# An attention in front of two feed-forward layers: scores in two rounds of 288 tokens beside pieces of v_m @ w_in, and attention groups tied between whole steps of the first product

## The chip, the cores and the metric

One core of one Trainium2 chip runs the whole program. The metric is device time in microseconds. Times are compared as medians of several runs. The profile is of one profiled execution; its times count from the start of its span.

## What is computed

Eight batches of eight heads, 576 tokens, head size 64, with 32 memory slots per head, go through an attention over the memory. The result, a matrix of 4608 tokens by 512, goes through two feed-forward layers with a hidden size of 2048.

```python
a = phi - np.max(phi, axis=2, keepdims=True); a = np.exp(a)
a = a / (np.sum(a, axis=2, keepdims=True) + 1e-09)
k_m = np.einsum('bhsm,bhsd->bhmd', a, k)
v_m = np.einsum('bhsm,bhsd->bhmd', a, v)
scores = scale * np.matmul(q, k_m.transpose(0, 1, 3, 2))
...
attn = attn / (np.sum(attn, axis=-1, keepdims=True) + 1e-09)
return np.matmul(attn, v_m).astype(np.float32)
...
h = x @ w_in; r = np.maximum(h, 0.0); g = r * r       # layer 1
h = x @ w_in; g = h * (1.0 / (1.0 + np.exp(-h)))      # layer 2
return (g @ w_out).astype(np.float32)
```

The layers' weights arrive as 64-bit words and are turned into fp32 on the chip.

## The kernel before, in words

The program has four stages, one after the other on TensorE: the attention with the first layer's `w_in` (lines up to L499, here called the front), then three large products that are not touched by the change: the first layer's `w_out` (L677), the second layer's `w_in` (L796) and its `w_out` (L677 again).

In the front, attention and `x @ w_in` are merged: since x is attn @ v_m per head, x @ w_in is attn @ (v_m @ w_in). So for each batch the kernel forms v_m @ w_in in four **pieces** of 512 hidden columns (`piece`, TensorE into `pswp` at L378) and multiplies them with the transposed attention `at`. That is the **first product** (`first_product`, into `h` at L482): 16 **steps** per batch, each one a block of 128 hidden units, 12 matmuls of 288 tokens (two halves of the 576 tokens by six). ScalarE evicts each step with a Relu into `gt` (L491). Two PSUM tiles `h` alternate.

While the 16 steps of one batch run, the attention of the next batch is done in small **groups** of matmuls between them, which here is called a cycle:

- the softmax over tokens of phi: `pm` (L316, two transposes for the maximum) and `psmx` (L325);
- k_m and v_m: `pskv` (L343, 40 matmuls 128 rows by 32 columns of the array, two groups of 20), then scaled and turned: `pst` (L365, two transposes twice) and copied to `kvm`;
- scores: `scores(r)` for rounds r = 0, 1, 2 of RT = 192 tokens: `pssc` (L378, 8 matmuls on 64 rows by 32 columns), then on VectorE two transposes of 32x32 blocks out of PSUM (L389), the row maximum, a subtraction, an exponential on ScalarE (L393), the sum, its reciprocal and the scaling (L397, on GpSimd from batch 1 on);
- `transpose_attn(r)`: a transpose (L406), the rounding to the upper part on ScalarE (L409), the rest by a subtraction (L410); the tile `et` between them has one buffer;
- the four pieces, `pswp`, split into an upper part by ScalarE (L420) and a rest by VectorE (L421).

All these small PSUM tiles come from one pool `bg` of two buffers. The `h` matmuls use the whole 128x128 array, as do `pm`, `psmx` and `pst`; the others use parts of it.

The order comes from two places. `PLAN` and `PLAN1` (L47 to L54) say ahead of which step each part is written, and a scheduler that runs when the program is built then moves instructions on each engine by its own simulated times. It may put a group into the middle of a step, or cut a group in two. On the chip each engine works through its list in order. `hold` ties the issue of background work to the start of a step.

Beside this, VectorE, ScalarE and the DMA queue of SyncE convert `w_out` of the first layer in the background (L146 to L198, tiles `st`, `pw`, `pp`), from step 20 on, one part per step; `g1` takes the outputs of the steps.

At the start, batch 0's attention has no first product to run beside; its three score rounds (all on VectorE, the first subtraction L410 on GpSimd) stand between the conversions of `w_in` (`unit`, L146 to L149).

Of the kernel before, what the change touches and what calls it, by code (L numbers as in the profile page):

```python
# [8 lines left out]
F32 = mybir.dt.float32  # L9
# [9 lines left out]
P = 128  # L19
# [3 lines left out]
NP = H // 2  # L23
HALF = S // 2
NF = DFF // P
NC = 5
NR = 3
RT = S // NR
# [18 lines left out]
PLAN = {  # L47
    "phi": -15, "kv": (-13, -11, -9, -7), "softmax": (-9, -6, -4), "product": (-1, 0), "turn": (2, 3),
    "q": (-5, -3, 6), "scores": (5, 7, 10), "attn": (7, 9, 12), "pieces": (5, 9, 13, 17),
}  # L50
PLAN1 = {
    "phi": -47, "kv": (0, 0, 1, 2), "softmax": (2, 4, 5), "product": (6, 7), "turn": (8, 9),
    "q": (3, 4, 10), "scores": (9, 11, 13), "attn": (11, 13, 15), "pieces": (10, 12, 14, 16),
}  # L54
# [15 lines left out]
def attention_moe_moe(ctx: ExitStack, tc, q, kv, phi, w_in1, w_out1, w_in2, w_out2, out):  # L70
# [18 lines left out]
    nc = tc.nc  # L89
# [24 lines left out]
    def hold(ins, until=10 ** 6, step=-1):  # L114

        if begun and len(begun) < until:
            after(ins, begun[step])

    def after(ins, other):
# [132 lines left out]
    def unit(j, i):  # L252
        ins = to_f32(win[:, j, 2 * i:2 * i + 2].rearrange("p k c -> p (k c)"), staged[j, i])
        if begun:
            hold(ins)
        elif j > 1:
            after(ins, ready[min(j, 4) - 2])

# [4 lines left out]
    def front(b):  # L263
# [26 lines left out]
        def load_q(r):  # L290
            if b == 0 and r == 2:
                t = gpool.tile([P, 2, S], F32, tag="gt", name="q")
                t = t.rearrange("p a n -> p (a n)")[:, :NP * RT].rearrange("p (k n) -> p k n", k=NP)
            else:
                t = fpool.tile([P, NP, RT], F32, tag="q", bufs=2, name="q")
            st["q", r] = t
            hold(nc.sync.dma_start(t, q[b, r]))
# [38 lines left out]
        def kv_product(g):  # L336

            ps = st["ps", g] = bank("pskv")[:, 0, :2 * D + 1]
            for c in range(NC):
                n = rows(c)  # L340
                for p in range(NP):
                    h = 2 * p + g
                    nc.tensor.matmul(  # L343
                        ps[p * M:(p + 1) * M], st["a"][:n, c, h * M:(h + 1) * M], st["kv"][:n, p, c, g],
                        start=(c == 0), stop=(c == NC - 1),
                    )

# [13 lines left out]
        def kv_turn(g):  # L361
            y = st["y", g]
            pst = st["pst", g] = bank("pst")[:, 0, :2 * P].rearrange("p (s n) -> p s n", s=2)
            for i in range(2):
                nc.tensor.transpose(pst[:, i], y[:, i].rearrange("p s d -> p (s d)"), ident)  # L365

            if g == 0:
                st["kvm"] = fpool.tile([P, 2, P], F32, tag="kvm", name="kvm")
            d = slice(g * D, (g + 1) * D)
            nc.vector.tensor_copy(st["kvm"][d], st["pst", g][d])  # L370

        def by_heads(ps, s, x):

            for g in range(2):
                d = slice(g * D, (g + 1) * D)
                for p in range(NP):
                    m = slice(p * M, (p + 1) * M)
                    nc.tensor.matmul(ps[m, g], st["kvm"][d, s, m], x(p)[d], start=True, stop=True)  # L378

# [76 lines left out]
        for g in range(2):  # L456
            at(begin + plan["product"][g], lambda g=g: (kv_product(g), kv_scale(g)))
            at(begin + plan["turn"][g], lambda g=g: kv_turn(g))
# [14 lines left out]
    def first_product(t):  # L473
# [4 lines left out]
        for half in range(2):  # L478
            tk = slice(half * HALF, (half + 1) * HALF)
            ops = [(g, s, x) for g in range(2) for s, x in ((0, 0), (0, 1), (1, 0))]  # L480
            for k, (g, s, x) in enumerate(ops):
# [4 lines left out]
                if half == k == 0:  # L486
                    begun.append(mm)
        if f % 2 == 0:
            gts[b] = gpool.tile([P, 2, S], F32, tag="gt", name="gt")
# [402 lines left out]
```

## Time and profile before

| | us |
|---|---|
| median of 3 runs (1430.03 to 1431.23) | 1431.19 |
| span of the profiled execution | 1426.6 |
| PE busy / DVE busy / ACT busy / POOL busy | 1377.4 / 1035.2 / 789.6 / 37.0 |
| front, up to the first matmul of L677 | 346.7 |
| mean granted TensorE clock | 0.996 |

The profile gives no time of its own for the profiled execution beyond the span; the runs' median is 4.6 us over that span. PE is TensorE's matmuls, DVE VectorE, ACT ScalarE, POOL GpSimd, SPq the DMA queue of SyncE. Matmuls overlap in the pipeline, so a row's duration is longer than the time until the next row starts; the distances between the starts of rows say what a group takes on TensorE. A matmul on fp32 data appears as two records where the program has one instruction (pssc x16 is a group of eight); the `h` matmuls on rounded fp32 appear once.

### The profile page before, as it was taken

What the parts mean: (1) busy time and instruction counts of PE and PEld (TensorE: products, weight loads), DVE (VectorE), ACT (ScalarE), POOL (GpSimd) and SP (SyncE); (2) the same over time, 40 slices, a digit from 0 to 9 for tenths busy, and PEclk for the clock granted to TensorE, in tenths of its full rate; (3) what the DMA queues carried; (4) which work ended last, traced back from release to release, by engine and by line L of the source; (5) the groups of instructions that cost most, each with busy time, mean ns of one, the idle gap of its engine ahead of it and who ended that gap; (6) DMA issues with size and microseconds to landing.
All of it is one profiled execution on the core that took longest, in us unless ns stands there. A gap on an engine that the chain in (4) does not pass through costs nothing.

```text
span 1426.6 us, 25453 instructions
## 1 busy us (share of the span) xinstructions
PE 1377.4 (97%) x9264; PEld 1305.5 (92%) x9264; DVE 1035.2 (73%) x1809; ACT 789.6 (55%) x1329; POOL 37.0 (3%) x52
## 2 busy tenths in 40 slices
PE   3899999999999999999999999999999999999999
PEld 1677878788899999999999999999998999999998
DVE  6867878772798978889957677566538768678583
ACT  3566666666767585775545455455444444444443
POOL 1210000000000000000000000000000000000000
PEclk9999999999999999999999999999999999999999
DMA  9769999889779787798998887888999575665740
GB/s 344 248 223 338 324 329 313 290 291 393 240 231 314 226 288 252 255 290 290 336 336 279 303 303 275 286 275 297 348 399 345 161 256 173 226 223 161 239 152 34
DMA packets 208829, 388.25 MB, mean 272 GB/s; under 512 B 19264, under 2 KB 91456, under 8 KB 208704
## 3 DMA queue, kind: packets, MB, share of 16 engines
q1 hardware_dynamic: 208704, 386.62, 80.0%
q8 instruction: 73, 1.20, 0.3%
q14 instruction: 52, 0.43, 0.1%
HBM read 253.38 MB, written 133.17 MB: 271 GB/s over the span
## 4 chain that ended last, share of the span: by engine, by line
PE 75%; DVE 10%; DMA 9%; ACT 3%; issue 2%; SPq 0%; POOL 0%; ACTq 0%; DVEq 0%; POOLq 0%
PE psa L677 21%; PE psa L796 14%; PE h L482 11%; PE psc L677 11%; PE psc L796 7%; PE psb L677 4%; PE psb L796 4%; DMA r<-g 3%; DVE c L649 3%; PE pswp L378 2%; DMA st<-moe_w_out 1%; PE pskv L343 1%; DMA ws<-w1o 1%; ACT c L648 1%; DVE r L642 1%
## 5 line engine op out<-in xcount | busy, mean ns | idle before, releaser
L649 DVE TENSOR_TENSOR c<-r,c 128x768 fp32r<-128x768 f32 x336 | 318.9, 958 | 162.4 <-ACT c L648 160.7
L677 PE MATMUL psa<-c,ws 128*128 128x384 f32 x2304 | 418.2, 339 | 11.4 <-DVE c L649 9.0
L677 PEld LDWEIGHTS psa<-c,ws 128*128 128x128 f32 x2304 | 405.1, 190 | 15.6 <-DVE c L649 12.3
L648 ACT CAST c<-r 128x768 fp32r<-128x768 f32 x336 | 277.4, 834 | 215.7 <-PE psa L677 106.9
L482 PEld LDWEIGHTS h<-at,wp 128*128 128x128 f32 x1536 | 209.3, 190 | 53.5 <-ACT gt L491 20.2
L482 PE MATMUL h<-at,wp 128*128 128x288 f32 x1536 | 230.0, 303 | 12.4 <-ACT at L409 7.9
L796 PE MATMUL psa<-xc,ws 128*128 128x384 f32 x1152 | 218.4, 336 | 0.0
L677 PE MATMUL psc<-c,ws 128*128 128x384 f32 x1152 | 207.0, 336 | 2.8 <-ACT c L648 2.8
L677 PEld LDWEIGHTS psc<-c,ws 128*128 128x128 f32 x1152 | 201.2, 188 | 3.1 <-ACT c L648 3.1
L796 PEld LDWEIGHTS psa<-xc,ws 128*128 128x128 f32 x1152 | 202.1, 188 | 0.6 <-ACT u L563 0.3
L491 ACT ACTIVATE gt<-h 128x576 f32<-128x576 f32 x128 | 82.4, 649 | 52.4 <-PE h L482 49.4
L796 PE MATMUL psc<-xc,ws 128*128 128x384 f32 x576 | 110.8, 335 | 0.0
L677 PE MATMUL psb<-c,ws 128*128 128x384 f32 x576 | 105.4, 337 | 1.2 <-DVE c L649 1.1
L186 ACT CAST pp<-pw 128x256 fp32r<-128x256 f32 x148 | 58.6, 404 | 85.3 <-DMA w2o<-pp 31.2
L677 PEld LDWEIGHTS psb<-c,ws 128*128 128x128 f32 x576 | 100.4, 188 | 2.6 <-DVE c L649 2.5
L796 PEld LDWEIGHTS psc<-xc,ws 128*128 128x128 f32 x576 | 100.8, 188 | 0.0
L624 ACT ACTIVATE r<-r 128x768 f32<-128x768 f32 x96 | 79.8, 844 | 30.9 <-DMA r<-g 29.6
L187 DVE TENSOR_TENSOR pp<-pw,pp 128x256 f32<-128x256 f32 x148 | 61.3, 421 | 45.1 <-ACT pp L186 43.9
L810 ACT ACTIVATE g2t<-g2t 128x1152 f32<-128x1152 f32 x48 | 55.0, 1163 | 29.4 <-DVE g2t L561 27.0
L146 ACT ACTIVATE pw<-st 128x256 f32<-128x256 f32 x96 | 40.5, 433 | 39.9 <-DMA st<-moe_w_out 22.3
L796 PE MATMUL psb<-xc,ws 128*128 128x384 f32 x288 | 56.7, 335 | 0.0
L563 ACT COPY u<-psa 128x384 f32<-128x384 f32 x72 | 33.7, 475 | 38.8 <-DVE g2t L561 25.1
(86 smaller groups left out, 1202.1 us busy)
## 6 DMA issues: line engine op xcount, KB each, us to landing
r<-g SPq DMA_DIRECT2D x192, 384.0 KB, 5.0
g<-g2t SPq DMA_DIRECT2D x48, 768.0 KB, 7.0
ws<-w2i SPq DMA_DIRECT2D x136, 256.0 KB, 5.0
ws<-w2o SPq DMA_DIRECT2D x136, 256.0 KB, 3.7
ws<-w1o SPq DMA_DIRECT2D x116, 256.0 KB, 4.7
g<-gt SPq DMA_DIRECT2D x64, 384.0 KB, 5.5
kv<-kv SPq DMA_DIRECT2D x32, 516.0 KB, 6.9
st<-moe_w_out SPq DMA_DIRECT2D x64, 256.0 KB, 4.8
```

The lines of the kernel that those rows point to most:

```text
L146: ins = nc.scalar.mul(f.bitcast(F32), w1.bitcast(F32), 2.0 ** -112)
L186: held(nc.scalar.copy(hi, w[:, of]))
L187: tt(lo, w[:, of], hi.bitcast(F32), op=ALU.subtract)
L482: mm = nc.tensor.matmul(h[:, half, :HALF], wp[b, j][:, g, s, fo:fo + P], attnT[b][:, x, g, tk], start=(k == 0), stop=(k == len(ops) - 1),)
L491: nc.scalar.activation(gt[:, f % 2].rearrange("p (h t) -> p h t", h=2), h[:, :, :HALF], AF.Relu)
L563: nc.scalar.copy(s("u1"), t["a"])
L624: nc.scalar.activation(raw[b, name, h], raw[b, name, h], AF.Square)
L648: nc.scalar.copy(c[:, 0], r(name))
L649: tt(c[:, 1], r(name), c[:, 0].bitcast(F32), op=ALU.subtract)
L677: mm = nc.tensor.matmul(ps[o][bank], W[h * QS + u][:, slot(n), wi, o * P:(o + 1) * P], x[:, xi, u], start=(n in FIRST and h == u == m == 0 ...
L796: mm = nc.tensor.matmul(ps[q][bank], W[q][:, slot(n), wi, k * P:(k + 1) * P], x[:, xi, k], start=(n in FIRST and k == 0 and m == 0), stop= ...
L810: nc.scalar.activation(gq[q][:, :3], gq[q][:, :3], AF.Silu)
```

## The change

Scores come in two rounds of 288 tokens instead of three of 192; 288 is also half of the first product's tokens. `PLAN` puts each round at the step of a piece (5 and 9), so that `scores` and `piece` are written one behind the other. For batches 2 and on, each group of the attention is tied by a dependency without a semaphore: its first matmul comes after the last matmul of the step before it, and the next step's first matmul comes after the group's last. So a tied group is neither cut nor put inside a step. `pm` and `psmx` are not tied. The load of q for batch 0 no longer borrows a `gt` tile, and the scratch for dynamic DMA in SBUF is set to 1024 bytes, which makes room for the larger q, e and et tiles.

```diff
-NR = 3
+NR = 2
 RT = S // NR
...
 PLAN = {
-    "phi": -15, "kv": (-13, -11, -9, -7), "softmax": (-9, -6, -4), "product": (-1, 0), "turn": (2, 3),
-    "q": (-5, -3, 6), "scores": (5, 7, 10), "attn": (7, 9, 12), "pieces": (5, 9, 13, 17),
+    "phi": -15, "kv": (-13, -11, -9, -7), "softmax": (-9, -6, -4), "product": (-1, -1), "turn": (3, 3),
+    "q": (-5, 3), "scores": (5, 9), "attn": (8, 12), "pieces": (5, 9, 13, 17),
 }
 PLAN1 = {
...
-    "q": (3, 4, 10), "scores": (9, 11, 13), "attn": (11, 13, 15), "pieces": (10, 12, 14, 16),
+    "q": (3, 4), "scores": (10, 12), "attn": (12, 14), "pieces": (10, 12, 14, 16),
 }
...
+    ended = []
+    between = []
+
+    def between_steps(mms):
+
+        first, last = mms[0], mms[-1]
+        follow(first, between[-1] if between else ended[-1])
+        between.append(last)
+
+    def follow(ins, other):
+        tc.add_manual_dep(
+            ins.ins, other.ins.name,
+            mybir.DependencyInfo(mybir.DependencyClass.NoSync, mybir.DependencyReason.SCHED_ONLY), reason="follow",
+        )
...
         def load_q(r):
-            if b == 0 and r == 2:
-                t = gpool.tile([P, 2, S], F32, tag="gt", name="q")
...
+            t = st["q", r] = fpool.tile([P, NP, RT], F32, tag="q", bufs=2, name="q")
...
+            if b > 1:
+                between_steps(mms)
...
                 if half == k == 0:
                     begun.append(mm)
+                    if between:
+                        follow(mm, between[-1])
+                        between.clear()
+        ended.append(mm)
...
-    nc = bacc.Bacc("TRN2", target_bir_lowering=False, num_devices=1)
+    nc = bacc.Bacc("TRN2", target_bir_lowering=False, num_devices=1, dynamic_dma_scratch_size=1024)
```

The call of `between_steps` stands in `kv_product`, `kv_turn` and `by_heads` (scores and pieces).

How the change moves instructions shows best on TensorE in a cycle of the middle of the front, at the scores and pieces. Names: `h` first product, `pssc` scores, `pswp` piece, `pm` phi's maximum. Before:

```order
L482 MATMUL h<-at,wp 128x288 x22
L378 MATMUL pssc<-q,kvm 32x192 x8
L482 MATMUL h<-at,wp 128x288 x12
L378 MATMUL pswp<-win,kvm 32x512 x5
L482 MATMUL h<-at,wp 128x288 x12
L378 MATMUL pswp<-win,kvm 32x512 x3
L482 MATMUL h<-at,wp 128x288 x12
L378 MATMUL pssc<-q,kvm 32x192 x8
L482 MATMUL h<-at,wp 128x288 x23
L316 MATMUL pm<-ident,m 128x128 x2
```

With the change, the same part of a cycle:

```order
L500 MATMUL h<-at,wp 128x288 x24
L393 MATMUL pssc<-q,kvm 32x288 x8
L393 MATMUL pswp<-win,kvm 32x512 x8
L500 MATMUL h<-at,wp 128x288 x48
L393 MATMUL pssc<-q,kvm 32x288 x8
L393 MATMUL pswp<-win,kvm 32x512 x8
L500 MATMUL h<-at,wp 128x288 x14
L326 MATMUL pm<-ident,m 128x128 x2
L500 MATMUL h<-at,wp 128x288 x34
```

The piece that was cut into 5 and 3 matmuls is whole, each round of scores stands straight before a piece, and one round is gone.

The second place is TensorE ahead of that, from k_m and v_m (`pskv`) to the turn (`pst`) and the first scores. Before:

```order
L343 MATMUL pskv<-kv,a 32x129 x40
L482 MATMUL h<-at,wp 128x288 x14
L378 MATMUL pswp<-win,kvm 32x512 x8
L482 MATMUL h<-at,wp 128x288 x10
L365 MATMUL pst<-ident,y_1534 128x128 x2
L482 MATMUL h<-at,wp 128x288 x24
L365 MATMUL pst<-ident,y_1581 128x128 x2
L378 MATMUL pssc<-q,kvm 32x192 x4
L482 MATMUL h<-at,wp 128x288 x14
L378 MATMUL pssc<-q,kvm 32x192 x4
L378 MATMUL pswp<-win,kvm 32x512 x8
```

With the change:

```order
L354 MATMUL pskv<-kv,a 32x129 x40
L500 MATMUL h<-at,wp 128x288 x24
L393 MATMUL pswp<-win,kvm 32x512 x8
L500 MATMUL h<-at,wp 128x288 x24
L377 MATMUL pst<-ident,y_1451 128x128 x2
L377 MATMUL pst<-ident,y_1478 128x128 x2
L500 MATMUL h<-at,wp 128x288 x24
```

The two turns stand together, the first scores are no longer cut in two by a stretch of the first product, and between the piece and the turns there are two whole steps.

## Rows read from the trace of the kernel before

**Rows 1.** The page's first part: busy time, share of the span, instructions.

```profile
PE 1377.4 (97%) x9264; PEld 1305.5 (92%) x9264; DVE 1035.2 (73%) x1809; ACT 789.6 (55%) x1329; POOL 37.0 (3%) x52
```

**Rows 2.** Busy time by stretch, four cycles of the front; the columns stand first.

```profile
core 0: us, PE busy (x) PEld busy (x) DVE busy (x) ACT busy (x) POOL busy (x), PEclk, DMA share, GB/s
...
164.50:202.38 37.88, 37.88 (x397) 30.50 (x396) 29.10 (x75) 23.11 (x46) 2.88 (x4) 1.00 0.99 344
...
240.20:279.07 38.87, 37.92 (x397) 30.48 (x396) 29.86 (x74) 24.17 (x50) 2.70 (x4) 1.00 0.87 279
sum 153.07, PE 151.52 PEld 121.87 DVE 119.80 ACT 95.58 POOL 11.06; mean PE 37.88 PEld 30.47 DVE 29.95 ACT 23.89 POOL 2.76
```

**Rows 3.** TensorE by time in one cycle: start, duration, engine, line, tile, count.

```profile
209.62 0.38 PE L365 MATMUL pst<-ident,y 128*128 128x128 f32 x2
209.75 3.43 PE L482 MATMUL h<-at,wp 128*128 128x288 f32 x24
213.03 0.38 PE L365 MATMUL pst<-ident,y 128*128 128x128 f32 x2
213.33 0.53 PE L378 MATMUL pssc<-q,kvm 64*32 64x192 f32 x8
213.79 2.13 PE L482 MATMUL h<-at,wp 128*128 128x288 f32 x14
215.85 0.37 PE L378 MATMUL pssc<-q,kvm 64*32 64x192 f32 x4
...
217.17 3.18 PE L482 MATMUL h<-at,wp 128*128 128x288 f32 x22
220.28 0.56 PE L378 MATMUL pssc<-q,kvm 64*32 64x192 f32 x16
220.76 1.85 PE L482 MATMUL h<-at,wp 128*128 128x288 f32 x12
222.54 1.07 PE L378 MATMUL pswp<-win,kvm 64*32 64x512 f32 x10
223.54 1.85 PE L482 MATMUL h<-at,wp 128*128 128x288 f32 x12
225.32 1.06 PE L378 MATMUL pswp<-win,kvm 64*32 64x512 f32 x6
226.31 1.85 PE L482 MATMUL h<-at,wp 128*128 128x288 f32 x12
...
235.79 1.09 PE L378 MATMUL pswp<-win,kvm 64*32 64x512 f32 x16
236.81 3.45 PE L482 MATMUL h<-at,wp 128*128 128x288 f32 x24
240.19 0.32 PE L343 MATMUL pskv<-kv,a 128*32 128x129 f32 x4
```

**Rows 4.** TensorE by time, scores straight ahead of a piece, batch 2's attention.

```profile
85.57 0.56 PE L378 MATMUL pssc<-q,kvm 64*32 64x192 f32 x16
85.97 1.09 PE L378 MATMUL pswp<-win,kvm 64*32 64x512 f32 x16
86.99 0.40 PE L482 MATMUL h<-at,wp 128*128 128x288 f32 x1
```

**Rows 5.** The start of the first product: VectorE and TensorE by time.

```profile
42.94 0.55 DVE L410 TENSOR_TENSOR at<-et,at 128x384 fp32r<-128x384 f32 x1
...
43.54 0.74 PEld L482 LDWEIGHTS h<-at,wp 128*128 128x128 f32 x3 [0.99 <-DVE at L410]
43.54 0.85 PE L482 MATMUL h<-at,wp 128*128 128x288 f32 x2 [0.64 <-DVE at L410]
```

**Rows 6.** Groups by line and shape from 126.06 to 279.0 us: busy, mean ns, idle before.

```profile
L491 ACT ACTIVATE gt<-h 128x576 f32<-128x576 f32 x65 | 41.9, 648 | 22.0 <-PE h L482 20.6 <-DMA g<-gt 1.0 <-ACT e L393 0.3
...
L421 DVE TENSOR_TENSOR wp<-pswp,wp 128x1024 fp32r<-128x1024 f32 x17 | 20.8, 1223 | 9.0 <-ACT wp L420 8.7
L420 ACT CAST wp<-pswp 128x1024 fp32r<-128x1024 f32 x16 | 16.1, 1005 | 3.4 <-PE pswp L378 3.4
...
L410 DVE TENSOR_TENSOR at<-et,at 128x384 fp32r<-128x384 f32 x12 | 6.6, 548 | 0.0
```

**Rows 7.** Waits of TensorE from 50 to 320 us: total, times, longest.

```profile
PE h L482 <- ACT gt L491: 2.1, 4, 0.9
PE pm L316 <- DVE m L309: 0.9, 1, 0.9
```

**Rows 8.** Busy time by stretch where the second stage's loads begin; columns as in Rows 2.

```profile
340.00:350.00 10.00, 8.16 (x49) 7.61 (x48) 3.29 (x4) 6.25 (x9) 0.00 (x0) 0.88 1.07 400
```

More of the change, by code (lines that the diff above doesn't have):

```diff
@@ L256, in unit @@
         elif j > 1:
-            after(ins, ready[min(j, 4) - 2])
+            after(ins, ready[min(j - 2, NR - 1)])
     wp = {}
@@ L290, in load_q @@
         def load_q(r):
-            if b == 0 and r == 2:
-                t = gpool.tile([P, 2, S], F32, tag="gt", name="q")
[L293 to L296, printed above, removed]
+            t = st["q", r] = fpool.tile([P, NP, RT], F32, tag="q", bufs=2, name="q")
             hold(nc.sync.dma_start(t, q[b, r]))
@@ L338, in kv_product @@
             ps = st["ps", g] = bank("pskv")[:, 0, :2 * D + 1]
+            mms = []
             for c in range(NC):
@@ L342, in kv_product @@
                     h = 2 * p + g
-                    nc.tensor.matmul(
+                    mms.append(nc.tensor.matmul(
                         ps[p * M:(p + 1) * M], st["a"][:n, c, h * M:(h + 1) * M], st["kv"][:n, p, c, g],
                         start=(c == 0), stop=(c == NC - 1),
-                    )
+                    ))
+            if b > 1:
+                between_steps(mms)
         def kv_scale(g):
@@ L363, in kv_turn @@
             pst = st["pst", g] = bank("pst")[:, 0, :2 * P].rearrange("p (s n) -> p s n", s=2)
-            for i in range(2):
-                nc.tensor.transpose(pst[:, i], y[:, i].rearrange("p s d -> p (s d)"), ident)
+            mms = [nc.tensor.transpose(pst[:, i], y[:, i].rearrange("p s d -> p (s d)"), ident) for i in range(2)]
+            if b > 1:
+                between_steps(mms)
             if g == 0:
@@ L372, in by_heads @@
         def by_heads(ps, s, x):
+            mms = []
             for g in range(2):
@@ L377, in by_heads @@
                     m = slice(p * M, (p + 1) * M)
-                    nc.tensor.matmul(ps[m, g], st["kvm"][d, s, m], x(p)[d], start=True, stop=True)
+                    mms.append(nc.tensor.matmul(ps[m, g], st["kvm"][d, s, m], x(p)[d], start=True, stop=True))
+            if b > 1:
+                between_steps(mms)
         def scores(r):
@@ L456, in front @@
         for g in range(2):
-            at(begin + plan["product"][g], lambda g=g: (kv_product(g), kv_scale(g)))
+            at(begin + plan["product"][g], lambda g=g: kv_product(g))
+            at(begin + plan["product"][g], lambda g=g: kv_scale(g))
             at(begin + plan["turn"][g], lambda g=g: kv_turn(g))
```

## The prediction

> **What bounds the kernel now.** I read the busy times first. TensorE is busy 97% of the span, VectorE 73%, ScalarE 55% [rows 1]. That alone could mislead, since a share is a mean over four stages, so the second view is the busy time by stretch in the stage that the change touches. There four cycles of the front (one cycle: 16 steps of the first product with the next batch's attention between them) last 153.07 us and TensorE is busy in 151.52 of them, 37.88 per cycle; VectorE has 29.95 of work per cycle and ScalarE 23.89 [rows 2]. So a cycle is as long as TensorE's own list, but for 1.55 us in four cycles. The waits say the same: in 270 us TensorE waited 2.1 us for evictions of the first product and 0.9 us for phi's maximum [rows 7]. The reader is to see that work taken off TensorE's list here shortens the front, as long as nothing else needs 37 us. One resource comes close: the DMA engines, with a share of 0.99 at 344 GB/s in one cycle, though 0.87 at 279 in another [rows 2].
>
> What does TensorE's list consist of? The time series answers [rows 3], if one takes distances between starts, not durations. Twelve matmuls of the first product that stand between two groups take 222.54 - 220.76 = 1.78 us; 24 in one stretch take 240.19 - 236.81 = 3.38. So a break in the first product costs 2 x 1.78 - 3.38 = 0.18 us by itself, whatever stands in it. Between two `pst`, 24 take 213.03 - 209.75 = 3.28. With no break they would take 3.38 - 0.18 = 3.20, so a break by a full-array group costs 0.08.
>
> **The change part by part**, per cycle, on the path since TensorE is the bound:
>
> 1. The cut piece becomes whole. It took 223.54 - 222.54 = 1.00 for 5 of its 8 matmuls and 226.31 - 225.32 = 0.99 for the other 3; a whole one takes 236.81 - 235.79 = 1.02 [rows 3]. Three matmuls cost as much as eight, because those on different parts of the array run side by side. Gain 0.97.
> 2. Breaks. A cycle before has 11: eight by groups on parts of the array, two by full-array groups (the first `pst`, `pm`), and one that the second `pst` shares with half a round of scores, at about the mean, 0.13. The order with the change has 7, five by groups on parts of the array and two by `pst` and `pm`. Three at 0.18 and the shared one go: 0.67. (In some cycles `psmx` stands apart from its piece; that is 0.08, left out.)
> 3. Scores. Before: a half round 213.79 - 213.33 = 0.46; the other half mixed with a piece, 217.17 - 215.85 = 1.32, less 1.02 for the piece, 0.30; two whole rounds at 220.76 - 220.28 = 0.48 [rows 3]. Sum 1.72. A round of 288 columns is not in the trace. A round of 192 straight ahead of a piece takes 85.97 - 85.57 = 0.40 [rows 4], which is the lower end; the upper end is that plus all that a piece of 512 has over a round of 192, 0.40 + 1.02 - 0.48 = 0.94. Both groups have eight matmuls of the same form, so I go by columns: 0.54 for 320 more, 0.16 for 96 more. Two rounds at 0.56 are 1.12, gain 0.60 (ends 0.92 and -0.16).
> 4. The second `pst` took 213.33 - 213.03 = 0.30 ahead of scores, the first 209.75 - 209.62 = 0.13 [rows 3]. Now both are followed by full-array work: gain 0.17.
>
> That is 2.41 per cycle. Six cycles are tied (attention of batches 2 to 7): 14.5. Behind them the order before cuts one of the last two pieces once more, into 3 and 5, the 3 straight behind another piece: 0.97 less one break that doesn't arise, 0.8. Sum 15.3. Batch 1's attention isn't tied; I leave its cycle at zero.
>
> On breaks the rows differ by which part of the array is used: 0.18 and 0.08. The Trainium skill (TensorEngine Tiling (Array Packing), Key Properties) says that changing the tiling mode drains TensorE, and another tile of the same mode doesn't. By that rule alone a `pst` among the first product would cost nothing; the trace has 0.08 there, and the measurement decides. The sum would be the same by either, but for the breaks by `pst` and `pm` that remain in it on both sides; the rule does agree with what rows 4 show, scores ahead of a piece of the same form 0.08 cheaper than ahead of the first product.
>
> **The start.** The first product's second half waits for VectorE's last subtraction of batch 0 and begins at 43.54 [rows 5]. VectorE does a round's passes over 384 columns there, one of which takes 0.548 us [rows 6]; the same kind of operation over 1024 takes 1.223, so 1.055 ns per column and 0.14 fixed. Going from three rounds to two saves the fixed part of about nine operations, 1.3 us, on the engine that TensorE waits for. Against it, the subtraction on GpSimd is half as long again, and `et` has one buffer, so the second round's transpose waits for it. I take -1.0, with ends 0 and -1.6.
>
> **Waits.** The tied order makes one place tighter. A piece's PSUM buffer is free after ScalarE's 1.005 and VectorE's 1.223 [rows 6], 2.2 us behind its last matmul. Before, the second `pst`, which needs that buffer, stood 4.6 us or more behind it (10 and 24 matmuls, 1.3 and 3.3); now 24 matmuls, 3.4, and a `pst` of 0.13. That leaves 1.3 us for whatever stands ahead in the two queues, and one long VectorE operation is 1.2. I allow 0.2 per cycle, +1.2 in all; ends 0 and 1.0 per cycle. Edits at nothing: the q loads carry the same bytes in fewer issues; GpSimd's scaling has 576 instead of 384 columns but GpSimd is busy 37 us in all [rows 1], and the transpose behind it is three steps off; VectorE loses the fixed part of eight operations a cycle, about 1.2, so its load falls from 29.95 to some 28.8 of 35.5, the same four fifths as before; the background's order is moved with the steps. The later stages shift as a whole, since their first loads are tied to steps.
>
> Sum: -15.3 - 1.0 + 1.2 = -15.1. The profiled execution has only its span, 1426.6; the runs' median is 4.6 above it, and I put the difference on that median: 1431.2 - 15.1 = 1416.1, rounded to **1416**.
>
> **Rivals.**
>
> *The DMA engines become the bound* (0.16). One cycle has a share of 0.99 at 344 GB/s; 37.88 x 344 is 13.0 MB, and in 35.5 us that needs 367 GB/s. If 0.99 is all they give for this mix, such a cycle stays at 37.9, and with three cycles that full some 7 us come back: 1423. Against it: 400 GB/s at a share of 1.07 where the second stage's loads begin [rows 8], so 344 x 1.07/0.99 = 372 is to be had, and the slack of the cycle with 0.87. What speaks for it: the mix there is other.
>
> *Eviction becomes the bound* (0.14). If each cycle's turn waits the whole length of one VectorE and one ScalarE operation more, about 0.8 per cycle instead of 0.2, the time is 1420. For it: the distance above falls from 4.6 to 3.5 us. Against: VectorE has a fifth of each cycle free. The Trainium skill has that as a rule (TensorEngine Tiling (Array Packing), PSUM Bottleneck): tiling speeds up TensorE and not the eviction of PSUM, which may become the bottleneck. By that rule the cycle would be set by the evictions; the trace so far shows TensorE never waiting for a piece's.
>
> *Waits go as well* (0.13). Of the 1.55 us in four cycles [rows 2] and the waits between 50 and 82 us nothing is left, as the new steps leave more room: 4 us less, the start at its better end: 1411.
>
> *Slower* (0.04). A step's `h` buffer must be evicted within the next step, 1.6 us when no group stands between; the eviction takes 0.648 [rows 6]. Before, groups spread through the steps gave ScalarE a break; now there are stretches of 48 matmuls without one. A pass of 1.005 ahead of the eviction makes 1.65, just beyond 1.6. Decisive is the mean delay ahead of the eviction: at 0.95 us it begins to cost, and from 1.15 on, each of the 96 tied steps loses over 0.2 and all of the gain is gone; at 0.25 per step, 24 us, the time is 1431.2 - 16.3 + 24 = 1439. Against it: such waits came to 2.1 us in 270 [rows 7], and ScalarE is busy 23.89 of a cycle [rows 2].
>
> That the change doesn't do what it says is no case: the order shows the groups whole.
>
> **How the numbers follow.** The forecast itself has 0.53. Its range, from the ends of the scores, the start and the waits, is about 1411 to 1421. Taking in most of the DMA and eviction cases above and the case without waits below gives **1408 to 1425**; outside are the slower case and both bounds together. A difference of 0.2%, 2.9 us, is about what a measurement of this kernel can tell from no change. Faster by more than that: 0.93, all but the slower rival and a sum of the first two. Within: 0.04. Slower by more: 0.03.
>
> **What would show it.** In the profile after: cycles of about 35.5 us with PE busy as long; pieces all of 16 records at 1.02 us; scores at about 0.56 ahead of them; stretches of 48 matmuls; the first matmul of the second stage near 331 instead of 346.7. It is wrong if cycles stay at 37 us or more, with idle time of TensorE ahead of `pst` or `pssc` (eviction), of `h` for `gt` (the slower case), or with DMA landings growing while the share stays at 1 (DMA). If the front ends 15 us earlier and the whole does not, the stage behind it waits for its loads.

## The result, and the profile after

The change makes the kernel slower, by about 1%. The median is 1442.9 us (1438.56 to 1451.42), and that of the kernel before in the same comparison 1431.2. The ratio of the two kernels' runs, which is not the quotient of these two medians, is 1.0098, with a 95% interval of 1.007 to 1.0127. Forecast were 1416 us and faster. The profiled execution spans 1441.0 us, 14.4 more than before.

The page's first part of the kernel after answers to [rows 1]: less busy time on TensorE, in a longer span.

```profile
PE 1370.5 (95%) x9136; PEld 1308.8 (91%) x9136; DVE 1032.5 (72%) x1736; ACT 788.0 (55%) x1313; POOL 35.0 (2%) x45
```

**TensorE's list became shorter, as forecast.** This is TensorE by time in a cycle of the kernel after, to be read against [rows 3] by the distances between starts.

```profile
188.44 0.60 PE L377 MATMUL pst<-ident,y 128*128 128x128 f32 x4
188.80 3.42 PE L500 MATMUL h<-at,wp 128*128 128x288 f32 x24
192.15 0.72 PE L393 MATMUL pssc<-q,kvm 64*32 64x288 f32 x16
192.66 1.06 PE L393 MATMUL pswp<-win,kvm 64*32 64x512 f32 x16
193.66 6.64 PE L500 MATMUL h<-at,wp 128*128 128x288 f32 x48
200.23 0.72 PE L393 MATMUL pssc<-q,kvm 64*32 64x288 f32 x16
...
209.78 1.09 PE L393 MATMUL pswp<-win,kvm 64*32 64x512 f32 x16
210.79 1.86 PE L500 MATMUL h<-at,wp 128*128 128x288 f32 x12
213.48 1.86 PE L500 MATMUL h<-at,wp 128*128 128x288 f32 x12 [0.82 <-ACT gt L513]
```

Pieces are whole: 193.66 - 192.66 = 1.00 behind scores, 210.79 - 209.78 = 1.01 alone (forecast 1.02). A round of 288 ahead of a piece takes 192.66 - 192.15 = 0.51 (forecast 0.56), the two turns 188.80 - 188.44 = 0.36, and 48 matmuls of the first product stand in one stretch. The last row shows the first sign of trouble: TensorE stood for 0.82 us with nothing to do but wait for `gt`.

**But it waits more.** Four cycles of the kernel after, by stretch, answer to [rows 2] (columns as there).

```profile
140.18:177.23 37.05, 35.75 (x379) 30.13 (x378) 28.95 (x64) 22.01 (x44) 2.49 (x3) 1.00 0.98 334
177.23:215.27 38.04, 36.09 (x380) 30.11 (x379) 31.58 (x68) 24.89 (x47) 2.62 (x3) 1.00 0.98 339
215.27:256.35 41.08, 37.54 (x379) 31.61 (x378) 31.83 (x69) 24.34 (x47) 2.49 (x3) 0.96 0.91 312
256.35:293.06 36.71, 35.76 (x379) 30.14 (x378) 28.02 (x63) 21.16 (x41) 2.49 (x3) 1.00 0.84 286
sum 152.88, PE 145.13 PEld 121.98 DVE 120.38 ACT 92.40 POOL 10.08; mean PE 36.28 PEld 30.50 DVE 30.10 ACT 23.10 POOL 2.52
```

The four cycles last 152.88 us instead of 153.07, with TensorE busy in 145.13 instead of 151.52: the list gave 6.4 us, and idle time went from 1.55 to 7.75. The longest cycle, 41.08, also had a granted clock of 0.96. The waits from 40 to 365 us (total, times, longest) answer to [rows 7]; first those of the kernel before in the same stretch.

```profile
PE h L482 <- ACT gt L491: 3.0, 6, 0.9
ACT pw L146 <- DMA st<-moe_w_out: 9.3, 8, 2.2
```

After:

```profile
PE h L500 <- ACT gt L513: 13.8, 8, 4.6
ACT pw L161 <- DMA st<-moe_w_out: 14.4, 6, 5.4
```

ScalarE waits in fewer places for the background's words of `w_out` (`st`), and longer in each; TensorE waits for ScalarE's evictions. The longest of these is spelled out by the three engines in time. SyncE's queue of the kernel after (start, time of the issue, what is moved):

```profile
105.51 0.35 SPq L307 DMA_DIRECT2D q<-q  x1
105.96 0.38 SPq L300 DMA_DIRECT2D kv<-kv  x1
106.43 0.90 SPq L520 DMA_DIRECT2D g<-gt  x2
109.12 1.09 SPq L149 DMA_DIRECT2D st<-moe_w_out  x2
```

ScalarE of the kernel after, and TensorE:

```profile
110.64 0.65 ACT L513 ACTIVATE gt<-h 128x576 f32<-128x576 f32 x1 [0.99 <-PE h L500]
116.70 0.43 ACT L161 ACTIVATE pw<-st 128x256 f32<-128x256 f32 x1 [5.40 <-DMA st<-moe_w_out]
117.03 0.99 ACT L437 CAST wp<-pswp 128x1024 fp32r<-128x1024 f32 x1
118.15 0.68 ACT L410 ACTIVATE e<-e 128x576 f32<-128x576 f32 x1
...
119.31 0.64 ACT L513 ACTIVATE gt<-h 128x576 f32<-128x576 f32 x1
```

```profile
111.99 3.45 PE L500 MATMUL h<-at,wp 128*128 128x288 f32 x24
120.01 2.29 PE L500 MATMUL h<-at,wp 128*128 128x288 f32 x8 [4.56 <-ACT gt L513]
```

The load of `st` is issued at 109.12, behind q, kv and g, and its conversion starts at 116.70. ScalarE works through its list in order, so the piece's eviction, the exponential and the eviction `gt` stand behind a conversion that nobody needs yet. TensorE runs its two free `h` tiles full and stops for 4.56 us. In the kernel before the same pair of loads was issued ahead of kv and q, and ScalarE waited a fifth as long:

```profile
99.45 0.82 SPq L134 DMA_DIRECT2D st<-moe_w_out  x2
...
101.31 0.54 SPq L285 DMA_DIRECT2D kv<-kv  x1
102.56 0.54 SPq L297 DMA_DIRECT2D q<-q  x1
```

```profile
102.57 0.44 ACT L146 ACTIVATE pw<-st 128x256 f32<-128x256 f32 x1 [0.96 <-DMA st<-moe_w_out]
```

**When it is lost.** The first product's steps can be compared one by one: the start of a step's first matmul in one trace, less that in the trace of before. At step 0 the kernel after is 1.0 us ahead, at step 8 1.1; at step 12 it is 5.7 behind, at 20 9.7, at 28 16.1, at 112 12.7, and at the first matmul of the next stage 16.3 (363.0 against 346.7). Two places therefore have to be explained: steps 8 to 20, where batch 1's attention ends and batch 2's begins and no words are converted yet, and the late words from step 20 on.

### The profile page after: what moved, and what is told of

It reads as the page before. It is cut to its first block, busy times and chain, and to the rows that moved or that the text cites. A ratio compares the mean times of both kernels' runs of the same rounds, so it can differ in the third digit from the quotient of the medians.

```text
span 1441.0 us, 25060 instructions
## 1 busy us (share of the span) xinstructions
PE 1370.5 (95%) x9136; PEld 1308.8 (91%) x9136; DVE 1032.5 (72%) x1736; ACT 788.0 (55%) x1313; POOL 35.0 (2%) x45
## 4 chain that ended last, share of the span: by engine, by line
PE 72%; DVE 11%; DMA 10%; ACT 3%; issue 2%; SPq 1%; POOL 1%; ACTq 0%; DVEq 0%; POOLq 0%
PE psa L699 22%; PE psa L818 12%; PE psc L699 12%; PE h L500 9%; PE psc L818 6%; PE psb L699 4%; PE psb L818 3%; DMA st<-moe_w_out 2%; DVE c L671 2%; DMA r<-g 2%; DMA g<-gt 1%; DMA w2i<-pp 1%; DMA st<-moe_w_in 1%; PE pskv L354 1%; PE pswp L393 1%
## 5 line engine op out<-in xcount | busy, mean ns | idle before, releaser
L699 PEld LDWEIGHTS psa<-c,ws 128*128 128x128 f32 x2304 | 403.4, 189 | 14.5 <-DVE c L671 11.4
L500 PEld LDWEIGHTS h<-at,wp 128*128 128x128 f32 x1536 | 215.4, 195 | 56.6 <-ACT gt L513 32.3
L500 PE MATMUL h<-at,wp 128*128 128x288 f32 x1536 | 232.7, 308 | 23.0 <-ACT gt L513 13.8
L818 PEld LDWEIGHTS psa<-xc,ws 128*128 128x128 f32 x1152 | 202.1, 188 | 0.9 <-ACT u L585 0.8
L162 DVE TENSOR_SCALAR pw<-pw 128x256 int32<-128x256 int32 x96 | 29.5, 316 | 38.9 <-ACT pw L161 38.1
```

The source lines that it names most:

```text
L162: nc.vector.tensor_scalar(f, f, 3, 0x7FFFFFFF, op0=ALU.logical_shift_left, op1=ALU.bitwise_and)
L500: mm = nc.tensor.matmul(h[:, half, :HALF], wp[b, j][:, g, s, fo:fo + P], attnT[b][:, x, g, tk], start=(k == 0), stop=(k == len(ops) - 1),)
L699: mm = nc.tensor.matmul(ps[o][bank], W[h * QS + u][:, slot(n), wi, o * P:(o + 1) * P], x[:, xi, u], start=(n in FIRST and h == u == m == 0 ...
L818: mm = nc.tensor.matmul(ps[q][bank], W[q][:, slot(n), wi, k * P:(k + 1) * P], x[:, xi, k], start=(n in FIRST and k == 0 and m == 0), stop= ...
```

## The experiments

Sixteen variants ran. "Lag" is the lag behind the profiled execution of the kernel before, as above; "28 to 112" is the time between these two steps (84 steps, 5.25 cycles; before 200.3 us). The kernel before had medians of 1428.6 to 1429.9 beside them. Each lag comes from one profiled execution, and executions of one kernel differ by several us (e14's took 1413.9 to 1419.5, and the profiled one was the fastest), so a difference of a few us between the lags of two kernels may be chance.

| run | us | ratio (95%) | lag at 12 | at 28 | 28 to 112 | lag at the front's end |
|---|---|---|---|---|---|---|
| the change | 1442.9 | 1.0098 [1.007, 1.0127] | 5.7 | 16.1 | 196.9 | 16.3 |
| e1 no ties | 1438.0 | 1.0062 [1.0042, 1.0082] | 6.2 | 7.7 | 202.1 | 8.4 |
| e2 before + ties | 1433.5 | 1.0025 [1.0007, 1.0042] | -0.6 | 5.8 | 198.4 | 6.3 |
| e3 two words early | 1440.8 | 1.0073 [1.0047, 1.0098] | 4.9 | 11.3 | 200.7 | 15.3 |
| e4 words ahead | 1429.2 | 0.9994 [0.9982, 1.0007] | 5.6 | 8.3 | 189.2 | -0.5 |
| e5 e4, batch 2 untied | 1430.6 | 1.0007 [0.9987, 1.0026] | 4.9 | 5.3 | 193.4 | 0.3 |
| e6 e4, phi later | 1428.5 | 0.9985 [0.9968, 1.0002] | 1.6 | 4.5 | 190.1 | -2.2 |
| e7 e4, own buffer | 1429.0 | 0.9998 [0.9982, 1.0015] | 8.4 | 7.4 | 189.2 | -1.3 |
| e8 e5 to e7 together | 1434.2 | 1.0028 [1.0011, 1.0045] | 7.5 | 9.7 | 193.2 | 4.3 |
| e9 before + words ahead | 1428.4 | 0.9993 [0.9976, 1.0009] | 0.5 | 2.5 | 198.8 | 1.0 |
| e10 e4, rounds 3,3,2,... | 1422.0 | 0.9942 [0.9924, 0.9959] | -0.6 | 2.2 | 189.3 | -7.0 |
| e11 e4, rounds 2,3,2,... | 1426.5 | 0.998 [0.9963, 0.9996] | 5.0 | 8.3 | 189.1 | -1.0 |
| e12 e10, phi later | 1424.0 | 0.997 [0.995, 0.9991] | -1.7 | 3.5 | 188.5 | -6.3 |
| e13 change, rounds 3,3,2,... | 1437.6 | 1.0067 [1.0035, 1.0098] | 1.1 | 5.9 | 204.5 | 12.8 |
| e14 e4, rounds 3,2,2,... | 1418.0 | 0.992 [0.9892, 0.9948] | -0.7 | -2.2 | 189.4 | -11.4 |
| e15 e10, batch 2 untied | 1424.1 | 0.9958 [0.9935, 0.9981] | 1.7 | 8.2 | 187.5 | -2.6 |
| e16 e10, no ties | 1428.4 | 0.9999 [0.9983, 1.0014] | 1.1 | 7.3 | 198.9 | 4.6 |

### Which part of the change, and the words (e1 to e4)

e1 takes the ties out of the change (`if b > 99` in place of `if b > 1` at the three calls of `between_steps`); e2 puts the ties, and nothing else, into the kernel before.

> Two rounds of 288 and the new plan, but no group is tied. By TensorE's own list (distances of starts as before) the front would be 4 us shorter than before the change. Theory A (on ScalarE's list the conversion of the background's w_out words stands ahead of evictions of the first product; the words land later than the build assumed, and TensorE, whose tied list has long stretches without a group, waits for the evictions): ScalarE's waits for the words fall to some 9 us in the front as before the change, TensorE's waits for gt to under 5 us; what stays is the loss of batch 1's part, up to step 20, about 6 to 10 us behind before: 1431 to 1436. Theory B (the DMA engines have no room for the same bytes in less time): waits for gt as with the ties wherever the share is 1, 1436 to 1443. Theory C (the ties themselves make TensorE stand still): all of the loss goes, 1427 or less.

> Three rounds of 192 and the plans as before the change; only the ties of batches 2 and on are added. By TensorE's own list the front would be 10.9 us shorter than before. Theory A: the first words of the background are loaded behind small q loads as before and land in 3 to 5 us, so the first long wait of ScalarE (5.4 us with the change) is under 2 us; steps 0 to 20 as before; waits of TensorE for gt 3 to 8 us in the front: 1422 to 1430. Theory B: the gain of the list comes back as waits, 1429 to 1433. Theory C: slower than before, 1435 or more.

Each half is slower than before by itself, by 0.62% and 0.25%, and in different places: e1 loses 6 us by step 12 and 2 behind it; e2 loses nothing by step 12, 4.7 us from there to step 20, and from step 28 to 112 it gains only 1.9 us with a shorter list, since it waits. Both times lie above the ranges that theory A gave. The waits of e2 from 40 to 365 us:

```profile
PE h L505 <- ACT gt L518: 9.6, 7, 2.3
ACT pw L161 <- DMA st<-moe_w_out: 12.7, 9, 3.5
```

e2 has the old order on SyncE's queue (words at 103.53 us, ahead of kv at 105.40 and q at 106.67). e1 has the new order and no ties, and waits 5.5 us for `gt` and 9.9 for words. So at least two causes were at work, and late words came more with the shorter list than with the new order of the queue.

e3 loads only the first two tiles of words earlier; e4 gives the words a third buffer and issues each load three tiles ahead of its conversion, through the whole front.

```diff
-        t = words_of[key, i] = prep.tile([P, 2 * P, 2], I32, tag="st", bufs=2, name="st")
+        t = words_of[key, i] = prep.tile([P, 2 * P, 2], I32, tag="st", bufs=3, name="st")
...
-            lambda: (convert(0), load(2)), lambda: split(0, 0), lambda: (convert(1), load(3)), lambda: split(1, 1),
-            lambda: convert(2), lambda: convert(3), lambda: split(6, 3), sums,
+            lambda: (convert(0), load_next(3)), lambda: split(0, 0), lambda: (convert(1), load_next(4)), lambda: split(1, 1),
+            lambda: (convert(2), load_next(5)), lambda: (convert(3), load_next(6)), lambda: split(6, 3), sums,
...
+            if t == WOUT0 - 8:
+                for i in range(3):
+                    load_words(("w1o", NQ - 1), src_out(w_out1, NQ - 1), i, hold)
```

(e3 has only the last three lines, with `range(2)`; `load_next` goes on to the next quarter's first tiles.)

> The change, with one thing moved: the first two tiles of w_out words are loaded 8 steps earlier (at step 12 and not at step 20 beside their conversion). Theory A: ScalarE's first wait for the words (5.4 us near 111) goes, with TensorE's 4.6 us for gt and the 6.8 us at half clock behind it; step 28 is 6 to 8 us earlier, and the whole 1433 to 1437. Theory B: the wait goes to another transfer (kv or q) of the same stretch, 1440 to 1443. Theory C: no difference, 1440 to 1445.

> As the run with the words early, and three buffers for the words of the front's background, each load 5 to 11 steps ahead of its conversion (3 to 5 steps with the change, since only two buffers). Theory A: ScalarE's waits for the words in the front fall from 14 us to under 3, TensorE's for gt from 13.8 to under 5, cycles of batches 3 to 6 come to 35.2 to 36.5 us; whole 1424 to 1432, what is left being batch 1's part and the half clock there. Theory B: the share of the DMA engines is 1 and cycles stay at 37 to 38, waits for kv, phi or the outputs instead, 1436 to 1442. Theory C: cycles as with the change, 1438 or more.

e3 removed the one wait it aimed at (lag at step 28 11.3 instead of 16.1) and lost it again later; at 1440.8 it is in the ranges of theories B and C and not of A. The waits of its profile from 40 to 365 us are as bad as with the change:

```profile
PE h L500 <- ACT gt L513: 14.3, 7, 3.3
ACT pw L161 <- DMA st<-moe_w_out: 19.6, 8, 4.7
```

With e4 the first loads are issued at 73 us, and the conversions start without a wait. From its SyncE queue, from ScalarE by time, and from its waits of TensorE in the same stretch:

```profile
73.01 2.80 SPq L149 DMA_DIRECT2D st<-moe_w_out  x3
```

```profile
109.56 0.42 ACT L161 ACTIVATE pw<-st 128x256 f32<-128x256 f32 x1
```

```profile
PE h L509 <- ACT gt L522: 3.0, 5, 1.4
```

That gives back 1442.9 - 1429.2 = 13.7 us, and the waits for `gt` are those of the kernel before again (3.0). The time is in theory A's range, and outside those of B (no room on the DMA engines) and C (the ties themselves). So the late words are shown as one cause. The Trainium skill (Trainium Kernel Development and Optimization, Best Practices) advises two buffers to overlap transfers with work; here the kernel had two, and with loads that took 7.6 us from 109.12 to 116.70 and steps of 1.6 us, two did not reach.

e9 puts the same words into the kernel before, as a control.

> The kernel before, unchanged but for e4's words (a third buffer, loads three tiles ahead) and the smaller ring for DMA descriptors that makes room for it. Theory A (late words cost time only where the first product runs faster than they land): the kernel before waits for gt for 3.0 us in all in its first product, so at most 3 us is to be had: 1427 to 1430 us. Rival (words on time are worth as much to any version): 1417 to 1422, and the change itself is worth nothing even with them.

It gains nothing that can be told (0.9993, 0.9976 to 1.0009). So here words ahead are worth something only where the first product runs fast enough to catch up with them. This run also has the smaller scratch for dynamic DMA, so that part of the change costs nothing that can be told.

### The start: four attempts that missed (e5 to e8)

With e4 the lag of 5.6 us at step 12 and 14.9 at step 16 was still there. Three edits were tried alone and together: ties from batch 3 on (`if b > 2`), the maximum of phi of batch 2 three steps later on VectorE (`"softmax": (-6, -4, -3)` for it), and a buffer of its own for that maximum (`tag="mp", bufs=1` in place of `tag="wlo"`, which it shares with GpSimd's passes).

> Words three tiles ahead as in e4_words_ahead (1429.2 us), and the ties hold for batches 3 to 7 only. With e4 the first product lay 14.9 us behind the kernel before at step 16, when its early batches were being scored, and was 0.5 us ahead at its end. Theory B (batch 2's tied groups stand on TensorE ahead of whole steps while their inputs are late, so that first-product work cannot fill the wait): the lag at step 16 falls to 6 us or less, and the time to 1421 to 1425 us. Rival C (the order on VectorE: the maximum of phi waits for its transfer ahead of the copies that batch 1's scores want): the ties don't matter, the lag at step 16 stays at 13 to 15, and the lost tying of one batch makes 1429 to 1432. Rival D (VectorE's maximum m of the first scores is held by GpSimd, whose buffer it shares): like C.

> As e4_words_ahead, and of batch 2 alone the maximum of phi is emitted at offset -6 instead of -9, so that on VectorE it stands behind the copies of batch 1's product. Theory C (VectorE's in-order wait for phi's transfer holds those copies): the waits of TensorE for kvm in the first 100 us (1.1 and 0.75 us with the change) go, as does the stretch at half clock near 74, the lag at step 16 falls by 3 to 5 us, and the time to 1424 to 1427. Rival B (ties of batch 2): no gain, 1428 to 1430. Rival D: no gain either.

> As e4_words_ahead, and the maximum m of the first scores has a buffer of its own instead of one that it shares with a pass on GpSimd. Theory D (that pass of 3.19 us at 47 to 50 us holds VectorE, and with it the first scores): batch 1's maximum at about 57 us comes 3 to 5 us sooner, the lag at step 8 falls by 2 to 4 us, the time to 1424 to 1427. Rivals B and C: what is gained is waited for again at batch 1's scores, 1428 to 1430.

> As e4_words_ahead with all three edits: ties from batch 3 on, batch 2's maximum of phi later, a buffer of its own for m. If the 14.9 us that the first product lost by step 16 came from the order of the first two batches (B, C and D together), most of it is back: lag at step 16 under 5 us, end of the first product 7 to 11 us ahead of the kernel before, 1418 to 1423 us. If it is the load on VectorE and the start as such that two rounds bring (rival), the lag moves to another wait, and the time stays within 1426 to 1430.

e5 did what its theory said at step 16, where the lag fell from 14.9 to 3.5, but by step 32 it was 8.8: the wait had only been moved. e6 took 4.0 us off the lag at step 12 and kept 1.7 of them to the front's end; 0.9985 (0.9968 to 1.0002) isn't told from no change by itself. e7 had batch 1's maximum finished at 52.8 instead of 56.9 us, and then TensorE waited for another of GpSimd's passes, which now came later. From its TensorE by time:

```profile
56.13 2.77 PE L509 MATMUL h<-at,wp 128*128 128x288 f32 x10 [4.75 <-POOL wp L455]
```

All three together are slower than e4 by 5.0 us. None of the three is the cause as it was put.

### The start: rounds of the first batches (e10 to e12, e14)

e10 lets each batch have its own number of rounds, three for batches 0 and 1 (with the kernel before's offsets for batch 1) and two with ties for the rest; e11 has three for batch 1 alone, e14 for batch 0 alone, e12 is e10 with e6's edit.

```diff
+ROUNDS = (3, 3) + (2,) * 6
...
+        nr = ROUNDS[b]
+        rt = S // nr
...
-            ps = bank("pssc")[:, :, :RT]
+            ps = bank("pssc")[:, :, :rt]
...
-            after(ins, ready[min(j - 2, NR - 1)])
+            after(ins, ready[min(j - 2, ROUNDS[0] - 1)])
```

(The other places with `RT` and `NR` likewise; q is laid out per batch.)

> As e4_words_ahead, but batches 0 and 1 score in three rounds of 192 with the offsets of the kernel before, batches 2 to 7 in two rounds with ties. Theory E (the start: a first round of 288 tokens makes batch 1's scores and copies late, and TensorE has no other work there yet): the lag at step 12 is under 2 us (e4: 5.6), at step 28 under 3 (e4: 8.3), the end of the first product 5 to 9 us ahead of the kernel before (e4: 0.5), 1420 to 1425 us. Rival F (batch 2's tied groups and the load of two batches on VectorE cost it, whatever the rounds): lag at step 28 as in e4, 7 to 9, and 1427 to 1430 us.

> As e10_rounds_3322 with batch 0 in two rounds again, so that only batch 1 differs from e4. Theory E with batch 1 as its place: as e10 within 1.5 us. If batch 0's rounds are its place: as e4, 1427 to 1430. Rival F: as e4 too, with e10 there as well.

> e10_rounds_3322 with e6's edit (batch 2's maximum of phi behind batch 1's copies on VectorE). By theory E the two are partly the same gain: 1418 to 1424 us, lag at step 28 1 to 3 us under e10's. Rival F: as e6, 1426 to 1429.

> As e10_rounds_3322 with batch 1 in two rounds, so that only batch 0 differs from e4. Batch 0's rounds as the place: the lag at step 12 is under 2 us and the time that of e10, 1420 to 1424 us. Rival (batch 1's rounds count too, each batch alone brings little): the time lies halfway or at e4's, 1425 to 1430.

The place is batch 0. With three rounds in it the lag at step 12 is -0.7 (e14) or -0.6 (e10), with two it stays at 5.6 (e4) or 5.0 (e11) whatever batch 1 does. Batch 1's two rounds cost nothing that can be told: e14 is at 1418.0 and e10 at 1422.0, with intervals that overlap. e12's phi edit adds nothing to e10. From step 12 to 20 e2, e4, e10 and e11 each lose 4 to 5 us more on the kernel before, and e14 none; why isn't shown.

**e14 beats both kernels**: 0.992 (0.9892 to 0.9948) of the kernel before. Its four cycles by stretch, to be read against those of the kernel after:

```profile
121.86:158.05 36.19, 35.82 (x380) 30.15 (x379) 29.50 (x64) 22.14 (x44) 2.44 (x3) 1.00 1.00 348
...
194.76:231.90 37.14, 35.68 (x379) 30.05 (x379) 31.40 (x69) 24.69 (x48) 2.48 (x3) 1.00 1.00 346
231.90:268.09 36.19, 35.83 (x379) 30.16 (x378) 28.64 (x65) 23.02 (x45) 2.43 (x3) 1.00 0.89 302
sum 146.23, PE 143.00 PEld 120.39 DVE 119.41 ACT 93.66 POOL 9.79; mean PE 35.75 PEld 30.10 DVE 29.85 ACT 23.41 POOL 2.45
```

146.23 against 153.07 before: 1.7 us per cycle. TensorE's busy time fell by 2.13 per cycle (37.88 to 35.75), and its idle time in the four cycles rose from 1.55 to 3.23.

How batch 0's rounds reach step 12 can be read, though e7 shows that no single link of it settles it. With two rounds (the kernel after) VectorE begins batch 1's maximum `m` behind a pass on GpSimd and ends it at 56.9 us; with three (e14) at 51.0. VectorE of the kernel after, then of e14:

```profile
50.38 0.95 DVE L314 TENSOR_TENSOR m<-a 128x256 f32<-128x256 f32 x1 [0.62 <-POOL wp L446]
...
56.45 0.41 DVE L319 TENSOR_TENSOR m<-m,a 64x256 f32<-64x256 f32 x1
```

```profile
46.95 0.41 DVE L331 TENSOR_TENSOR m<-a 128x256 f32<-128x256 f32 x1
...
50.04 0.95 DVE L336 TENSOR_TENSOR m<-m,a 64x256 f32<-64x256 f32 x1
```

All that hangs on it in batch 1's attention (the maximum over rows, the exponentials, k_m and v_m, the scores) comes later; that this chain makes the 5.7 us is argued, not shown. What would hold against two rounds in batch 0 with another order of pieces and conversions wasn't tried, and stays open.

### Is it independent, and what are the ties worth (e13, e15, e16)

e13 has e10's rounds without e4's words; e15 is e10 with ties from batch 3 on, e16 e10 without any.

> The change with batches 0 and 1 in three rounds, words as the change has them (two buffers, no earlier load). If the two causes, late words and batch 0's and 1's two rounds, are independent, 7.3 us come back, as from e4 to e10: 1434 to 1437 us, with ScalarE still waiting 12 us or more for words. Rival (TensorE waits for the later of the two, so mending one alone brings little): 1439 to 1443.

> As e10_rounds_3322 with ties from batch 3 on. The lag of 7.6 us that e10 has at step 16 and the 3.5 at step 20 fall to under 3; the untied pieces and scores of batch 2 cost about 2.4 us by the forecast's sum. If batch 2's ties hold up TensorE where its inputs are late, 1418 to 1421 us; if not, what is gained at step 16 is given back by step 32 as with e5, 1422 to 1425.

> As e10_rounds_3322 without any ties: what the rounds are worth alone when words and start are on time. By the forecast's parts, the whole pieces (.97 us a cycle) and the breaks (.67) hang on the ties, the scores (.60) on the rounds, the transposes (.17) on both being tied: the stretches of 16 steps after step 28 are 0.4 to 0.8 us shorter than before's, against about 2 with ties, and the time is 1425 to 1429 us. Rival (ties are worth nothing on the chip, since idle TensorE time swallows them): as e10, 1421 to 1423.

e13 came out at 1437.6, a little above what independence said (1434 to 1437): 5.3 us less than the change, where the same edit gives 7.2 from e4 to e10. The intervals of e13 and the change overlap, so the independence of the two causes isn't settled by it. In its profile the waits for words are longer than with the change: from 40 to 365 us ScalarE waits 19.9 us for them (14.4 with the change) and TensorE 15.8 for `gt` (13.8).

e16 answers what is real in the forecast's sum. Without ties the 84 steps take 198.9 us, with them 189.3 (e10), and the kernel before with timely words 198.8 (e9). So with two rounds the ties give 9.6 us in 5.25 cycles, 1.8 per cycle, and two rounds without ties give nothing. Ties with three rounds and timely words weren't run, but e2's trace has TensorE's list with ties and three rounds. By stretch, the 84 steps of e2 and of e10 (columns as in [rows 2]):

```profile
123.70:322.14 198.44, 191.36 (x2035) 158.28 (x2034) 155.24 (x386) 125.45 (x245) 14.20 (x20) 0.99 0.91 312
```

```profile
120.01:309.31 189.30, 185.62 (x1952) 156.44 (x1950) 155.07 (x340) 122.61 (x233) 13.39 (x15) 1.00 0.95 329
```

TensorE is busy 191.36 us with three rounds and 185.62 with two. Some 1.5 of the difference is 3.4 us that e2 spent at the lower clock, so two rounds and the plan that goes with them are worth an estimated 4 us here, 0.8 per cycle, once the groups are tied. e15 shows again that batch 2's ties hold nothing up: untied, the lag is 6.0 at step 16 instead of 7.6, but 8.2 instead of 2.2 at step 28 (its step 0 began 2.0 us later than e10's).

## Why the prediction was wrong, point by point

- **The sum of the list was nearly right.** Forecast 2.41 us per cycle, less 0.2 for waits: 2.2. With words and start mended, TensorE's busy time falls by 2.13 per cycle, and the 84 steps take 189.4 us (e14) instead of 200.3; without the 0.8 for the pieces at the end (below) that is 1.9 per cycle, and 1.6 against the kernel before with timely words (e9). Whole pieces and breaks are where they were put. Two turns take 0.36 together against 0.30 + 0.13 before, a gain of 0.07 and not 0.17, and two rounds of scores 1.02 against 1.72, a gain of 0.70 and not 0.60. Without the ties two rounds gained nothing (e16).
- **The step that failed first: "the background's order is moved with the steps", put among the edits at nothing.** The conversions move with the steps, but the loads they need move only as far ahead of them as two buffers let them, and on SyncE's queue they now stand behind q, kv and g. A faster cycle and a queue in another order made the words late, the first more than the second (e2 against e1), and ScalarE's list turned that into most of TensorE's 13.8 us of waiting for `gt`, and into time at the lower clock (below). The prediction did count what moves on SyncE ("the same bytes in fewer issues") and didn't ask what is issued behind it. Measured: 13.7 us (e4).
- **The second: "Batch 1's attention isn't tied; I leave its cycle at zero", with "the start" at -1.0.** Step 0 does come about a us sooner (36.1 against 37.2 us; over all traces, two rounds in batch 0 begin step 0 at 34.7 to 36.7, three at 36.3 to 38.7). But the prediction followed the start only to its first matmul. Behind it, batch 0's two rounds move VectorE's and GpSimd's other work, and batch 1's attention is 5.7 us late by step 12. Measured: 1429.2 - 1418.0 = 11.2 us (e4 to e14; 7.2 from e4 to e10).
- **Waits on evictions** were forecast at 0.2 per cycle. In e14's four cycles idle time rose by 0.42 per cycle, twice that and within the ends of 0 and 1.0. The largest part, 1.8 us (waits from 120 to 340 us), is the second `pskv`, another group than the `pst` that it was put at, waiting for a piece's eviction (below). VectorE's work per cycle stayed at 29.85 us, where 28.8 was forecast.

```profile
PE pskv L371 <- DVE wp L455: 1.8, 2, 1.1
```

- **The whole pieces at the end**, 0.8, came as forecast, ahead of step 112. Before, two pieces took 1.85 us from 308.69 (eight matmuls and three) and 1.00 from 313.91 (the other five), 2.85 together; in e14 those at 299.23 and 306.83 take 1.02 each. From step 112 to the end of the front e14 then loses 1.7 us on before; the largest part is a wait of 1.59 for `gt` at 316.08, behind ScalarE's wait of 2.31 for a load of the next stage (`r`).
- **The rivals.** *DMA as the bound*: no; e14's cycle with a share of 1.00 at 348 GB/s takes 36.19 us, as long as one with 0.89 at 302. It was not how much the DMA engines carry but when one load lands. *Eviction*: not as the bound, but the waits for a piece's eviction above are of its kind, and larger than the sum had them. *Waits go as well*: no, idle time grew. *Slower*: forecast at 0.04 and 1439 us; the place was right, TensorE waiting for `gt`, and the price near, but the mechanism wrong. It isn't 96 steps with a little each, behind a pass of 1.005; it is eight waits, five of which (10.35 of the 13.8 us, the longest 4.56) come right behind a conversion that waited for its words, and one of 2.00 behind the load of `r`. The profile of before had the row that speaks of it, ScalarE's 9.3 us of waiting for words, and the prediction didn't show it: it looked at the waits of the engine that bounds, and not at those of the engine that it depends on.
- **The range.** e14's 1418.0 us lies in the forecast's range, but that is another kernel: it has words issued earlier and batch 0 in three rounds. It doesn't make the forecast right.

## What to carry to other kernels

Before shortening the list of the engine that bounds, look for the waits of the engines that feed it or clear its buffers: a wait for a transfer that is covered today stands in an in-order list ahead of work that is needed at once, and a faster list uncovers it. When a change of tile size touches the first of several batches, follow the start past the first result to the second batch. If a change that should pay doesn't, mend the waits it uncovered before giving it up: here the same change with words issued earlier and batch 0 left alone gives 0.992.

## What the runs showed of the hardware that was not expected

TensorE's clock fell in the front after quite short waits. In the kernel before, the granted clock was 1.00 (2.4 GHz) from 47 us to the front's end; in the kernel after five stretches ran at the lower of the two levels (1.2 GHz, 0.50). By stretch (columns as in [rows 2]): the front from 47.2 us on, before and after, then of the kernel after two of the stretches at the lower level and the sum of all five.

```profile
47.20:346.70 299.50, 292.55 (x3004) 236.59 (x2990) 212.51 (x511) 186.07 (x361) 29.72 (x38) 1.00 0.89 303
```

```profile
47.20:363.00 315.80, 288.08 (x2890) 240.76 (x2889) 213.23 (x450) 185.25 (x349) 29.37 (x33) 0.96 0.85 288
```

```profile
93.80:100.60 6.80, 5.83 (x59) 4.50 (x60) 2.68 (x7) 1.92 (x5) 0.00 (x0) 0.50 0.00 0
117.70:124.50 6.80, 4.49 (x19) 4.49 (x20) 6.77 (x16) 4.03 (x9) 1.16 (x1) 0.50 0.76 249
...
sum 23.90, PE 20.59 PEld 17.81 DVE 12.41 ACT 10.87 POOL 4.33; mean PE 4.12 PEld 3.56 DVE 2.48 ACT 2.17 POOL 0.87
```

Shortly ahead of the first of the two the engine had waited 1.78 us for an exponential, and it waited 0.97 for a piece's eviction early in it; the second begins inside the wait of 4.56 us shown above. Not every such wait was followed by a fall: in e14 waits of 1.09 and 1.59 us in the front were not. TensorE by time in the first of the two:

```profile
97.88 3.07 PE L500 MATMUL h<-at,wp 128*128 128x288 f32 x12
100.88 0.66 PE L393 MATMUL pswp<-win,kvm 64*32 64x512 f32 x8
```

A step's 12 matmuls took 100.88 - 97.88 = 3.00 us; at the full clock 48 take 200.23 - 193.66 = 6.57, a quarter of which is 1.64. So a wait here can cost more than its length. An estimate of how much: if all 20.59 us of work in the five stretches were slowed as this step was, they cost some 9 us. e4 has two such stretches behind 47 us, with 9.54 us of work (some 4 us), and e14 none in its front. By that, about 5 of the 16.8 us between the lags of the change and of e4 at the front's end are clock, and about 4 of the 10.9 between e4 and e14; the rest is waiting and TensorE's list.
